# A gated two-branch linear-attention kernel: the raw K and Q weights loaded by one queue in the order of the fold steps

## The chip, the cores and the metric

The kernel runs on one core of a Trainium2 chip. Five engines work side by side, each through its own list of instructions in program order: TensorE (PE, matrix products into PSUM; PEld are its weight loads), VectorE (DVE), ScalarE (ACT), GpSimd (POOL) and SyncE (SP, which here only issues transfers). They meet at semaphores. Transfers are issued by SyncE or GpSimd, each into a queue of its own, and carried out by 16 DMA engines. The metric is the time of one execution in microseconds (us), taken as the median of several runs.

## The reference

Two attention branches A and B work on the same x, and a gate mixes their outputs. S is 2048, the model width 448, with 16 heads of 28. Cut to what matters:

```python
def branch(x, wqkv, w_phi, wo):
    q, k, v = split(x @ wqkv)                    # 16 heads of 28
    pq = einsum("bhsd,hdf->bhsf", q, w_phi)      # the same for pk with k
    phi_q = concat([softmax(pq), softmax(-pq)])  # the same for phi_k
    kv = einsum("bhsf,bhsd->bhfd", phi_k, v)
    z = einsum("bhsf->bhf", phi_k)
    num = einsum("bhqf,bhfd->bhqd", phi_q, kv)
    den = einsum("bhqf,bhf->bhq", phi_q, z) + 1e-6
    return (num / den).reshape(B, S, D) @ wo

g = sigmoid((x * gate_w).sum(-1, keepdims=True))
return g * branch(x, A...) + (1 - g) * branch(x, B...)
```

## The kernel before

**Tiling.** The 2048 rows are 16 tiles of 128; x arrives transposed in eight pairs of tiles. Every float32 operand of a projection is split into a high part (rounded to the matmul's input format) and a low part (what is left), and a projection of one tile and one branch is 11 matmuls: four of high by high, four of high x by low weight, three of low x by high weight. ACT (or GpSimd) makes the high part, VectorE or GpSimd the low part by a subtraction.

**Folding.** The feature map applies `w_phi` to q and k. The kernel multiplies `w_phi` into the K and Q weights once, at the start. That takes four fold steps n = 0 to 3: branch b = n // 2, and in it half gh of the heads. A step is 32 small matmuls into the PSUM tile F (line 357), a transpose of F by VectorE into the buffer `ft0` (in `ret`) for even n or `ft1` (in `ru`) for odd n (line 362), and then for K and for Q two high parts by ACT and two low parts by VectorE or GpSimd, into `rk` and `rq`. F is one buffer, so step n + 1 needs the transpose of step n; and the transpose of step n + 2 needs all eight parts of step n to be read.

**The raw K and Q weights** (`in_wkt`, `in_wqt`: 448 columns, of which the host repeats the last 64 to make 512) are loaded into `wts`, a view of `ret` with 28 of each 32 partitions in use. `load_wt(k, b)` loads both halves of a branch in four transfers, one for each group of 32 partitions: two are issued by SyncE, two by GpSimd. The branch B half of `wts` lies where the raw V weights (`wvr`) are, so it waits until these are split.

**The start.** TensorE runs some warm-up matmuls, then V of tiles 0 and 1 (line 441, `v_first`), which takes the parts of x pair 0 and of the V weights as they arrive. V of tile 1 goes into the PSUM tile K, for want of another. Then V of tiles 2 to 4 (line 409) is interleaved with the four fold steps, and K and Q of tile 0 follow. From there on a steady pattern of K, Q, V, the accumulation of kv, and later the output stage fills TensorE to the end.

**What sets the order.** `steps()` is a list by hand; it gives TensorE's order. All other instructions are placed by `Plan.order`: a list scheduler that takes, for the engine free next, the ready step with the earliest due time. A due time follows backwards from the steps that need it, less a handicap `ahead` that some steps are given. SyncE may have eight transfers under way: a ninth waits for the semaphore of the one eight places before it. Steps marked `two` are those of VectorE or GpSimd that the plan does not let run beside one of the other engine. Only the order is kept: on the chip each engine runs through its list and waits at semaphores.

The lines of the prediction's steps: 290 to 302 load and split x pair 0; 319 to 329 the V weights; 341 to 348 `load_wt`; 350 to 371 `fold`; 453 to 459 `v_out`, which evicts V and reads the gate column `glog`; 666 to 678 `later`, which hands the fold buffers over.

## Time and profile before

| | us |
|---|---|
| median of the 3 runs | 347.61 |
| lowest, highest run | 343.46, 347.83 |
| profiled execution, its own time | 345.97 |
| its span, first to last instruction | 344.2 |
| TensorE busy in the span | 333.1 (97%) |
| VectorE busy | 285.1 (83%) |
| GpSimd busy | 251.5 (73%) |
| ScalarE busy | 143.7 (42%) |

Busy times are of one profiled execution. A TensorE that is 97% busy need not be at its best, since a matmul counts as busy from its start to its modelled end, and they overlap: the distance from start to start says what one costs. A wait in brackets in the rows of a timeline is the time in which that engine stood idle just before, and what ended it.

### The profile page before, as it was taken

The page shows a single profiled execution, that of the slowest core. Times are in us where ns is not written, and L with a number is a line of the kernel's source. Part 1 is how long each engine was busy: PE and PEld are TensorE (multiplying, and loading weights), DVE is VectorE, ACT ScalarE, POOL GpSimd, SP SyncE. Part 2 cuts the span into 40 slices and gives each one's busy share as a digit, 9 for nine tenths or more (in the row PEclk, how much of TensorE's full clock was granted, in tenths as well). Part 3 has the DMA queues.
Part 4 walks back from the last instruction along what each step waited for, and adds up shares of the span by engine and source line. Part 5 has one row for each costly group of instructions (what it writes and reads, how often), then busy time and mean ns, then how long its engine had stood idle before and what let it go on. Part 6 is the DMA issues. An engine that isn't in the chain of part 4 may idle for free.

```text
span 344.2 us, 8900 instructions
## 1 busy us (share of the span) xinstructions
PE 333.1 (97%) x3776; PEld 296.5 (86%) x3776; DVE 285.1 (83%) x338; ACT 143.7 (42%) x219; POOL 251.5 (73%) x211
## 2 busy tenths in 40 slices
PE   7889899999999999999999999999999999999995
PEld 6777587999999999999999999899878888788894
DVE  4608886997779769899998999997599999999960
ACT  4516743553444535364444452343043243433231
POOL 8426605899999799999996998697087778788500
PEclk9999989999999999999999999999999999999999
DMA  7995620550317756964735422376974545141011
GB/s 251 251 206 133 203 75 1 156 168 2 116 55 261 252 169 229 327 204 197 246 84 236 143 55 81 96 248 261 301 259 164 202 152 183 76 177 55 29 53 53
DMA packets 29262, 55.18 MB, mean 160 GB/s; under 512 B 4472, under 2 KB 23528, under 8 KB 26920
## 3 DMA queue, kind: packets, MB, share of 16 engines
q1 hardware_dynamic: 28328, 52.68, 47.6%
q0 software_dynamic: 896, 1.95, 2.6%
q8 instruction: 29, 0.48, 0.6%
q14 instruction: 9, 0.07, 0.1%
HBM read 32.00 MB, written 24.22 MB: 163 GB/s over the span
## 4 chain that ended last, share of the span: by engine, by line
POOL 30%; PE 24%; DVE 23%; DMA 10%; issue 8%; ACT 2%; SPq 1%; POOLq 0%; DVEq 0%; ACTq 0%
POOL ret L266 20%; PE O L630 10%; DVE ret L545 5%; DMA ret<-in_wqt 4%; PE K L409 3%; POOL rx L266 3%; PE Q L409 3%; DVE rv L593 3%; POOL rv L602 3%; PE N L582 2%; DVE sm L488 2%; DVE mx L481 2%; DVE qsm L540 2%; DMA wst<-wos 1%; DMA ret<-in_wv 1%
## 5 line engine op out<-in xcount | busy, mean ns | idle before, releaser
L409 PE MATMUL K<-rk,rx 128*128 128x432 f32 x352 | 74.0, 366 | 0.7 <-ACT pk L269 0.6
L409 PE MATMUL Q<-rq,rx 128*128 128x432 f32 x352 | 72.4, 360 | 0.2 <-DVE Q L672 0.2
L409 PEld LDWEIGHTS K<-rk,rx 128*128 128x128 f32 x352 | 67.1, 192 | 5.1 <-ACT pk L269 1.5
L630 PE MATMUL O<-rk,rx 128*128 128x448 f32 x336 | 70.6, 369 | 0.1
L630 PEld LDWEIGHTS O<-rk,rx 128*128 128x128 f32 x336 | 62.5, 188 | 8.5 <-ACT rx L621 1.2
L409 PEld LDWEIGHTS Q<-rq,rx 128*128 128x128 f32 x352 | 65.9, 188 | 4.4 <-PE K L409 0.7
L269 ACT ACTIVATE ret<-ret 128x896 f32<-128x896 f32 x48 | 45.7, 953 | 55.0 <-POOL ret L266 54.9
L266 POOL TENSOR_TENSOR ret<-ret,sm 128x896 f32<-128x896 f32 x32 | 53.9, 1707 | 8.1 <-DVE sm L489 8.1
L266 POOL TENSOR_TENSOR ret<-pk,mx 128x896 f32<-128x896 f32 x16 | 27.3, 1705 | 16.6 <-DVE mx L481 16.5
L488 DVE TENSOR_REDUCE sm<-ret 128x32 f32<-128x896 f32 x32 | 33.8, 1073 | 6.7 <-ACT ret L269 6.7
L545 DVE STREAM_TRANSPOSE ret<-ret 128x2048 f32<-128x2048 f32 x16 | 36.5, 2282 | 1.9 <-POOL ret L266 1.6
L540 DVE TENSOR_REDUCE qsm<-ret 128x32 f32<-128x896 f32 x32 | 33.4, 1055 | 3.0 <-ACT ret L269 2.7
L409 PE MATMUL VA<-rv,rx 128*128 128x450 f32 x154 | 34.7, 372 | 0.3 <-POOL rx L266 0.3
L409 PE MATMUL VB<-rv,rx 128*128 128x448 f32 x154 | 33.7, 366 | 0.0
L266 POOL TENSOR_TENSOR ret<-qmn,ru 128x896 f32<-128x896 f32 x16 | 28.2, 1765 | 5.3 <-DVE ret L545 4.2
L269 ACT ACTIVATE ret<-ru 128x896 f32<-128x896 f32 x16 | 15.2, 952 | 39.4 <-issue 17.3
L409 PEld LDWEIGHTS VA<-rv,rx 128*128 128x128 f32 x154 | 28.5, 189 | 3.6 <-POOL rx L266 0.7
L409 PEld LDWEIGHTS VB<-rv,rx 128*128 128x128 f32 x154 | 28.8, 188 | 3.0 <-issue 0.4
L266 POOL TENSOR_TENSOR ret<-mx,pk 128x896 f32<-128x896 f32 x16 | 27.3, 1706 | 1.5 <-DVE mx L482 1.5
L266 POOL TENSOR_TENSOR ret<-ret,qsm 128x896 f32<-128x896 f32 x16 | 27.3, 1705 | 0.9
L602 POOL TENSOR_TENSOR rv<-rv,rd 128x896 f32<-128x896 f32 x14 | 23.8, 1703 | 1.1
L534 DVE TENSOR_REDUCE qmn<-ru 128x32 f32<-128x896 f32 x16 | 16.9, 1058 | 6.7 <-DMA ru<-qd 6.6
(94 smaller groups left out, 445.1 us busy)
## 6 DMA issues: line engine op xcount, KB each, us to landing
ed<-ret SPq DMA_DIRECT2D x8, 1024.0 KB
ret<-ed SPq DMA_DIRECT2D x8, 1024.0 KB
qd<-ru SPq DMA_DIRECT2D x64, 112.0 KB
ru<-qd SPq DMA_DIRECT2D x16, 448.0 KB
out<-ret SPq DMA_DIRECT2D x16, 224.0 KB
wod<-wst SPq DMA_DIRECT2D x14, 224.0 KB
rk<-wod SPq DMA_DIRECT2D x2, 1568.0 KB
xraw<-in_xt SPq DMA_DIRECT2D x6, 512.0 KB
```

The lines of the kernel that those rows point to most:

```text
L266: return lambda: ENG[eng].tensor_tensor(val(o), val(a), val(b), op)
L269: return lambda: A.activation(val(o), val(i), f, **k)
L409: nc.tensor.matmul(bank[name][:, k, lo:hi], x[:, xc, o:o + P], w[l][:, c], start=i == 0, stop=i == len(XT) - 1)
L481: put("DVE", 2 * D, lambda: V.tensor_reduce(mh[0], pkh, AX.X, OP.max), [kp], [km[0]])
L488: put("DVE", 2 * D, lambda s=s, e3=e3: V.tensor_reduce(sm[:, s], e3, AX.X, OP.add), [ke[s]], [("sm", t % 2, s)])
L534: put("DVE", 2 * D, lambda: V.tensor_reduce(qmn, tq.rearrange("p c b g f -> p c (b g) f"), AX.X, OP.min), [kt], [kn])
L540: put("DVE", 2 * D, lambda s=s, e3=e3: V.tensor_reduce(qsm[:, s], e3, AX.X, OP.add), [ke[s]], [("qsm", i, s)])
L545: add("DVE", 2.25, lambda: V.transpose(eTf[slot], eq.rearrange("p s a c f -> p (s a c f)")), ke, turned(slot))
L582: nc.tensor.matmul(bank["N"][32 * g:32 * g + 32, r, 2 * b * P:2 * b * P + 2 * P], kvt[32 * r:32 * r + 32, b, s, g], eTp[slots[0] // 2][32 ...
L593: add("DVE", 0.07 + 1.08 * nt, lambda: V.transpose(ctr().rearrange("p (r n) -> p r n", r=4), bank["N"][:, :, :2 * nt * P]), ["N"], [("ctr" ...
L602: put(eng, 2 * D, lambda: ENG[eng].tensor_tensor(mid["o", n % 3].rearrange("p (c a f) -> p a c f", c=4, a=8), ctv()[:, :, i, :, :DH], rd[: ...
L630: nc.tensor.matmul(bank[pb][:, 0, :D], a, w, start=i == 0, stop=i == len(terms) - 1)
```

## The change

It has five parts.

1. `load_wt` loads one fold step instead of one matrix of one branch: eight transfers (four groups of partitions in the order 0, 2, 1, 3, in each K and then Q) of 28 partitions, two heads' rows and 448 columns, all issued by SyncE. There are 32 of them where there were 16, and GpSimd issues none.
2. The 64 repeated columns are no longer loaded. GpSimd copies them, one copy for each step (`COPY ret<-ret`), which waits for all eight transfers of the step; the fold waits for the copy. Two memsets at the start clear those columns in the partitions that no transfer writes.
3. The V weights are loaded branch by branch (all of A, then all of B), by large `ahead` values; the low part of x pair 0 that GpSimd made goes to VectorE.
4. TensorE's order: each fold step comes one V group earlier, and V of tile 4, branch B, goes behind the first K.
5. The q low parts of all four steps go to GpSimd ("DP" in all); VectorE had those of steps 2 and 3. The transposes of all steps and the gate column of tiles 0 and 1 get an `ahead`; the `two` marks are set otherwise.

```diff
-    yield from (("V01", 0, 0, 1), ("x1",), ("V01", 1, 0), ("V01", 1, 1), ("wq", 0), ("x", 2), ("wq", 1), ("V", 2), ("F", 0, 0, "DP"), ("V", 3, 0), ("F", 0, 1, "DP"))
...
+    yield from (("V01", 0, 0, 1), ("x1",), ("V01", 1, 0), ("V01", 1, 1), ("wt", 0), ("x", 2), ("wt", 1), ("wt", 2), ("wt", 3), ("V", 2, 0), ("F", 0, "DP"), ("V", 2, 1))
...
-    def low_part(eng, n, o, a, h, r, w):
-        put(eng, n, tt(eng, o, a, h, OP.subtract), r, w, two=eng == "DVE")
+    def low_part(eng, n, o, a, h, r, w, **k):
+        put(eng, n, tt(eng, o, a, h, OP.subtract), r, w, two=True, **k)
...
-        low_part("POOL", 4 * P, t[:, 5:7], xraw[:, 1:3], f[:, 1:3], [("x0raw", 1), ("x0h", 1), ("x0h", 2)], [("x0l", i) for i in (1, 2)])
+        low_part("DVE", 4 * P, t[:, 5:7], xraw[:, 1:3], f[:, 1:3], [("x0raw", 1), ("x0h", 1), ("x0h", 2)], [("x0l", i) for i in (1, 2)], ahead=140.0)
...
-        add("SP", 0.4, dma(wvr[:, c, lo:hi], wv[c * P:(c + 1) * P, lo:hi]), [], [("wvr", c, b)], lat=2.5, kb=331, ahead=50.0 if c + b == 0 else 30.0 - 2 * (c + 4 * b))
+        add("SP", 0.4, dma(wvr[:, c, lo:hi], wv[c * P:(c + 1) * P, lo:hi]), [], [("wvr", c, b)], lat=2.5, kb=331, ahead=8000.0 if c + b == 0 else 6000.0 - 500 * (c + 4 * b))
...
-    def load_wt(k, b):
-        rows = (wkt, wqt)[k][b].rearrange("(q g d) c -> q d g c", q=4, d=DH)
-        for q in range(4):
-            o, i, w = wts[32 * q:32 * q + DH, k, b], rows[q], [("wt", k, b, q)]
-            if q < 2:
-                add("SP", 0.2, dma(o, i), [], w, lat=2, kb=690)
-            else:
-                add("POOL", 0.6, lambda o=o, i=i: G.dma_start(o, i), [("vh", 2, 1)], w, lat=4 + 1.3 * (4 * b + 2 * k + q - 2), ahead=8.0 if b == 0 else 0.0)
+    def load_wt(n):
+        b, gh = divmod(n, 2)
+        for q in (0, 2, 1, 3):
+            for k in range(2):
+                i = (wkt, wqt)[k][b].rearrange("(q l g d) c -> q g d l c", q=4, l=2, d=DH)[q, gh, :, :, :D]
+                o = wts[HP * q:HP * q + DH, k, b].rearrange("p (l g) c -> p g l c", l=2)[:, gh, :, :D]
+                add("SP", 0.33, dma(o, i), [], [("wt", k, n, q)], lat=2, kb=180, ahead=100.0 - 30 * n)
+        t = wts[:, :, b].rearrange("p k (l g) c -> p g k l c", l=2)[:, gh]
+        put("POOL", 256, lambda: G.tensor_copy(t[:, :, :, D:], t[:, :, :, 3 * P:D]), [("wt", k, n, q) for k in range(2) for q in range(4)], [("wd", n)], two=False, ahead=6.0)
...
-        add("PE", 1.4, mm, [("wpd",), *[("wt", k, b, q) for k in range(2) for q in range(4)]], ["F"])
+        add("PE", 1.4, mm, [("wpd",), ("wd", n), *[("wt", k, n, q) for k in range(2) for q in range(4)]], ["F"])
...
-            add("ACT", 0.2, act(glog[:, t:t + 1], lambda: bank[n_][:, k, D:D + 1], AF.Exp, scale=-1.0), [kb], [("gl", t)])
+            add("ACT", 0.2, act(glog[:, t:t + 1], lambda: bank[n_][:, k, D:D + 1], AF.Exp, scale=-1.0), [kb], [("gl", t)], ahead=9.0 * (t < 2))
...
+    for b in range(2):
+        first("POOL", 0.3, lambda b=b: G.memset(wts[:, :, b, :, 3 * P:D] if b == 0 else wts[:, 1, 1, 3, 3 * P:D], 0.0),
+              wt0 if b == 0 else [("wt", 1, 3, q) for q in range(4)])
```

What the plan makes of it, at three places. First TensorE's list from V of tile 2 to the second K, before. VA and VB are V of branches A and B, F is a fold step, K and Q are the projections; x11 is one group.

```order
L409 MATMUL VA<-rv,rx 128x450 x11
L409 MATMUL VB<-rv,rx 128x448 x11
L357 MATMUL F<-ret,wpd 32x256 x32
L409 MATMUL VA<-rv,rx 128x450 x11
L357 MATMUL F<-ret,wpd 32x256 x32
L409 MATMUL VB<-rv,rx 128x448 x11
L409 MATMUL VA<-rv,rx 128x450 x11
L357 MATMUL F<-ret,wpd 32x256 x32
L409 MATMUL VB<-rv,rx 128x448 x11
L357 MATMUL F<-ret,wpd 32x256 x32
L409 MATMUL K<-rk,rx 128x432 x11
L409 MATMUL Q<-rq,rx 128x432 x11
```

The same place in TensorE's list after the change:

```order
L410 MATMUL VA<-rv,rx 128x450 x11
L358 MATMUL F<-ret,wpd 32x256 x32
L410 MATMUL VB<-rv,rx 128x448 x11
L410 MATMUL VA<-rv,rx 128x450 x11
L358 MATMUL F<-ret,wpd 32x256 x32
L410 MATMUL VB<-rv,rx 128x448 x11
L358 MATMUL F<-ret,wpd 32x256 x32
L410 MATMUL VA<-rv,rx 128x450 x11
L358 MATMUL F<-ret,wpd 32x256 x32
L410 MATMUL K<-rk,rx 128x432 x11
L410 MATMUL VB<-rv,rx 128x448 x11
L410 MATMUL Q<-rq,rx 128x432 x11
```

One group of V stands ahead of the first fold step instead of two, one between steps 1 and 2 and between steps 2 and 3, and the last V group stands between the first K and the first Q.

Second, SyncE's list from x pair 1 (`ret<-in_xt`) to x pair 3, before. `in_wkt` and `in_wqt` are the raw K and Q weights, `xraw<-in_xt` x pairs 2 and 3; DMAHW0 to 7 are the semaphores of its eight places.

```order
L272 DMA ret<-in_xt 128x4x256 [waits DMAHW2_49]
L272 DMA ret<-in_wkt 28x4x512 [waits DMAHW3_49]
L272 DMA ret<-in_wkt 28x4x512 [waits DMAHW4_49]
L272 DMA ret<-in_wqt 28x4x512 [waits DMAHW5_49]
L272 DMA ret<-in_wqt 28x4x512 [waits DMAHW6_49]
L272 DMA xraw<-in_xt 128x4x256 [waits DVE_49,DMAHW7_49,Activation_49,Pool_49]
L272 DMA ret<-in_wkt 28x4x512 [waits DMAHW0_49,DVE_49]
L272 DMA ret<-in_wkt 28x4x512 [waits DMAHW1_49]
L272 DMA ret<-in_wqt 28x4x512 [waits DMAHW2_49,DVE_49]
L272 DMA ret<-in_wqt 28x4x512 [waits DMAHW3_49]
L272 DMA xraw<-in_xt 128x4x256 [waits DMAHW7_49,DMAHW4_49,Pool_49]
```

SyncE's list after the change, from x pair 1 to the first transfer of fold step 1; 23 more of the same kind follow, and then x pair 3:

```order
L272 DMA ret<-in_xt 128x4x256 [waits DMAHW2_49]
L272 DMA ret<-in_wkt 28x2x448 [waits DMAHW3_49,Pool_49]
L272 DMA ret<-in_wqt 28x2x448 [waits DMAHW4_49]
L272 DMA ret<-in_wkt 28x2x448 [waits DMAHW5_49]
L272 DMA ret<-in_wqt 28x2x448 [waits DMAHW6_49]
L272 DMA ret<-in_wkt 28x2x448 [waits DMAHW7_49]
L272 DMA ret<-in_wqt 28x2x448 [waits DMAHW0_49]
L272 DMA ret<-in_wkt 28x2x448 [waits DMAHW1_49]
L272 DMA ret<-in_wqt 28x2x448 [waits DMAHW2_49]
L272 DMA xraw<-in_xt 128x4x256 [waits DMAHW3_49,DVE_49,Activation_49]
L272 DMA ret<-in_wkt 28x2x448 [waits DMAHW4_49]
```

Ahead of x pair 2 stands one fold step instead of half a branch, the rest behind it; the last transfer of step 0 waits for DMAHW2, the semaphore of x pair 1.

Third, GpSimd's list from the splits of x pair 1 to the first q low parts, before (`rx<-ret` is x pair 1, `rx<-xraw` x pair 2, `rq` are q low parts; DMASW are the semaphores of its own queue):

```order
L266 TENSOR_TENSOR rx<-ret,rx 64x128 [waits DMAHW2_49,Activation_49,Pool_49]
L348 DMA ret<-in_wqt 28x4x512 [waits DMAHW4_49,DMAHW5_49,DMAHW1_49,DMAHW6_49,DMASW4_49,DVE_49]
L348 DMA ret<-in_wqt 28x4x512 [waits DMASW5_49]
L348 DMA ret<-in_wkt 28x4x512 [waits DMAHW3_49,DMAHW7_49,DMAHW0_49,DMASW6_49]
L348 DMA ret<-in_wkt 28x4x512 [waits DMASW7_49]
L266 TENSOR_TENSOR rx<-ret,rx 128x3x128 [waits Pool_49]
L314 CAST rx<-xraw 128x1024 [waits DMAHW7_49]
L266 TENSOR_TENSOR rx<-xraw,rx 64x256 [waits Pool_49]
L266 TENSOR_TENSOR rx<-xraw,rx 128x768 [waits Pool_49]
L678 MEMSET ret 128x64x4 [waits DMAHW5_49,DMASW1_49,DMAHW6_49,DMASW0_49,PE_49]
L678 MEMSET ret 128x64x4 [waits DMAHW3_49,DMAHW4_49,DMASW3_49,DMASW2_49]
L266 TENSOR_TENSOR rq<-ret,rq 128x2x8x27 [waits DVE_49,Activation_49]
```

GpSimd's list after the change, from the second split of x pair 1:

```order
L266 TENSOR_TENSOR rx<-ret,rx 128x3x128 [waits Pool_49]
L349 COPY ret<-ret 128x4x64 [waits DMAHW4_49,DMAHW5_49,DMAHW3_49,DMAHW6_49,DMAHW2_49,DMAHW7_49,DMAHW1_49,DMAHW0_49]
L314 CAST rx<-xraw 128x1024 [waits DMAHW3_49]
L266 TENSOR_TENSOR rx<-xraw,rx 64x256 [waits Pool_49]
L266 TENSOR_TENSOR rx<-xraw,rx 128x768 [waits Pool_49]
L349 COPY ret<-ret 128x4x64 [waits DMAHW4_49,DMAHW5_49,DMAHW3_49,DMAHW6_49,DMAHW2_49,DMAHW7_49,DMAHW1_49,DMAHW0_49]
L266 TENSOR_TENSOR rq<-ret,rq 128x2x8x27 [waits DVE_49,Activation_49]
L349 COPY ret<-ret 128x4x64 [waits DMAHW4_49,DMAHW5_49,DMAHW3_49,DMAHW6_49,DMAHW2_49,DMAHW7_49,DMAHW1_49,DMAHW0_49]
L266 TENSOR_TENSOR rq<-ret,rq 128x2x8x27 [waits Activation_49]
L683 MEMSET ret 128x64x4 [waits PE_49,Pool_49]
L683 MEMSET ret 128x64x4
L349 COPY ret<-ret 128x4x64 [waits DMAHW4_49,DMAHW5_49,DMAHW3_49,DMAHW6_49,DMAHW2_49,DMAHW7_49,DMAHW1_49,DMAHW0_49]
```

The transfers are gone from it, and the copies of steps 0 to 3 stand between its splits and the q low parts, each waiting for all eight semaphores of SyncE's places.

44 lines of the change are left out of this document (22 added, 22 removed).

## The prediction

> **What bounds the kernel now.** I read the busy time by stage first, then TensorE's timeline through the stage that the change touches, then who is late there. The stage view gives a stretch and its length, the busy time of TensorE, its weight loads, VectorE (DVE), ScalarE (ACT) and GpSimd (POOL), the granted TensorE clock, the DMA share and GB/s.
>
> ```profile
> 5.59:17.51 11.92, 9.89 (x53) 8.15 (x46) 8.14 (x13) 6.62 (x14) 7.32 (x14) 1.00 1.06 280
> 52.86:340.30 287.44, 286.99 (x3286) 258.98 (x3286) 252.79 (x302) 116.40 (x173) 227.29 (x173) 1.00 0.47 158
> ```
>
> From 52.86 to 340.30 TensorE is busy for 286.99 of 287.44 us: nothing is to be had there except by starting it earlier. What can be won lies ahead of it. In TensorE's timeline (start, length, what, in brackets the wait before it) VA and VB hold V of the two branches, and F is a fold step:
>
> ```profile
> 5.59 0.47 PE L441 MATMUL VA<-rv,rx 128*128 128x450 f32 x1
> ...
> 9.05 0.47 PE L441 MATMUL VA<-rv,rx 128*128 128x450 f32 x1 [1.13 <-DVE rv L266]
> ...
> 15.14 2.53 PE L441 MATMUL K<-rv,rx 128*128 128x448 f32 x11 [0.74 <-ACT glog L269]
> 17.51 2.40 PE L409 MATMUL VA<-rv,rx 128*128 128x450 f32 x11
> 19.74 2.38 PE L409 MATMUL VB<-rv,rx 128*128 128x448 f32 x11
> 22.06 0.61 PE L357 MATMUL F<-ret,wpd 28*32 28x256 f32 x2
> 23.54 1.69 PE L357 MATMUL F<-ret,wpd 28*32 28x256 f32 x62 [0.86 <-DMA ret<-in_wqt]
> 25.15 2.50 PE L409 MATMUL VA<-rv,rx 128*128 128x450 f32 x11
> ...
> 35.73 2.49 PE L409 MATMUL VB<-rv,rx 128*128 128x448 f32 x11
> 39.88 1.49 PE L357 MATMUL F<-ret,wpd 28*32 28x256 f32 x64 [1.66 <-DVE ret L362]
> 41.31 3.98 PE L409 MATMUL K<-rk,rx 128*128 128x432 f32 x11
> 45.51 2.40 PE L409 MATMUL Q<-rq,rx 128*128 128x432 f32 x11 [0.23 <-DVE Q L672]
> 47.75 0.36 PE L409 MATMUL K<-rk,rx 128*128 128x432 f32 x1
> ```
>
> Starts are pipelined, so prices go from start to start. Eleven V matmuls cost 19.74 - 17.51 = 2.23, say 2.25; a fold step 41.31 - 39.88 = 1.43; eleven K or Q matmuls 47.75 - 45.51 = 2.24. From 5.59 to 47.75 stand ten groups of V (four of them for tiles 0 and 1), four fold steps, one K and one Q: 22.5 + 5.7 + 4.5 = 32.7 us of work in 42.16 us. So 9.5 us are lost, 2.9 in the first V stage (11.92 for 9.0) and 6.6 behind it. That is the ceiling of any gain: 345.97 - 9.5 = 336.5.
>
> **Where the 6.6 sit.** Fold step 0 took 25.15 - 22.06 = 3.09, 1.66 too much, for a Q weight that had not landed. Fold step 3 came 1.9 late (39.88 - 35.73 - 2.25), since the transpose ahead of it waited for GpSimd. The next K took 4.20 instead of 2.24. The rest is small pieces.
>
> ```profile
> 29.08 1.04 POOL L314 CAST rx<-xraw 128x1024 fp32r<-128x1024 f32 x1 [9.79 <-DMA xraw<-in_xt]
> ```
> ```profile
> 37.51 2.32 DVE L362 STREAM_TRANSPOSE ret<-F 128x2048 f32<-128x2048 f32 x1 [1.26 <-POOL rq L266]
> ```
>
> GpSimd sat 9.79 us for x pair 2 (tiles 4 and 5), whose transfer stood among the fold weights, so its q low parts came late, and the transpose could not overwrite what they still read. The root is the order and speed of the transfers:
>
> ```profile
> 6.00:11.00 5.00, 3.71 (x18) 2.77 (x17) 4.45 (x6) 3.48 (x6) 4.72 (x9) 1.00 1.07 363
> 11.00:13.00 2.00, 2.00 (x11) 1.85 (x10) 1.25 (x3) 0.99 (x4) 0.00 (x0) 1.00 1.05 200
> 11.00:29.00 18.00, 16.39 (x189) 13.02 (x187) 5.60 (x8) 6.16 (x15) 3.92 (x6) 1.00 1.02 210
> 29.00:31.00 2.00, 2.00 (x18) 1.81 (x11) 1.90 (x2) 2.00 (x5) 1.84 (x2) 1.00 0.84 168
> ```
>
> **The change part by part: transfers.** Loads over 128 partitions ran at 363 GB/s up to 11 us; fold weights and x pair 2 at 210, the DMA engines full (share 1.02); the tail, with few transfers left, at 168 (0.84). The change loads 448 of 512 columns: 32 transfers of 28 x 2 x 448 x 4 bytes = 100 KB, 3.21 MB instead of 3.67, all from SyncE, in the order step 0 (0.80 MB), x pair 2 (0.52), steps 1, 2, 3. What SyncE's queue reaches alone is not shown. I bound it by 168 and 210 and take 210: a share of 1.02 says that the engines, not the number of queues, set it, and at 200 (11 to 13) it was no different. Counted from 11.0: step 0 at 14.8, x pair 2 at 17.3, step 1 at 21.1, step 2 at 24.9, step 3 at 28.8. Only step 0 is held up: its last transfer reuses the semaphore of x pair 1.
>
> ```profile
> 13.88 1.15 ACT L269 ACTIVATE rx<-ret 128x512 fp32r<-128x512 f32 x2 [0.37 <-DMA ret<-in_xt]
> ```
> ```profile
> 8.09 0.93 SPq L272 DMA_DIRECT2D ret<-in_wqt  x2
> ...
> 33.47 0.39 SPq L272 DMA_DIRECT2D xraw<-in_xt  x1
> ```
>
> x pair 1 landed at 13.88, so that transfer is issued at 14 and lands near 16. An issue costs 0.93 / 2 = 0.47; the 25 behind it take 11.7 us, to 25.7, less than the transfers. x pair 3 and the output weights stand behind them on SyncE; they were issued from 33.47 on, and the queue now reaches them before 29. The prices that follow are from the view of one tile (count, then min/median/max in ns):
>
> ```profile
> L266 DVE TENSOR_TENSOR rv<-ret,rv x8: 618/624/2172, 4.8 to 13.0; 128x450 fp32r<-128x450 f32 x4, 128x448 fp32r<-128x448 f32 x4
> ...
> L269 ACT ACTIVATE rk<-ret x4: 937/968/1007, 28.1 to 40.7; 128x432 fp32r<-128x432 f32 x4
> L266 DVE TENSOR_TENSOR rk<-ret,rk x4: 920/1062/1821, 29.1 to 44.4; 128x432 fp32r<-128x432 f32 x4
> ...
> L266 POOL TENSOR_TENSOR rx<-ret,rx x2: 573/792/1012, 15.2 to 18.3; 64x128 fp32r<-64x128 f32 x1, 128x384 fp32r<-128x384 f32 x1
> ...
> L678 POOL MEMSET ret<- x2: 312/313/314, 33.4 to 33.6; 128x256 f32 x2
> L266 POOL TENSOR_TENSOR rq<-ret,rq x2: 1575/1814/2052, 33.9 to 35.4; 128x432 fp32r<-128x432 f32 x2
> ```
>
> The eight transfers taken off GpSimd were issued ahead of its wait of 9.79 us: what they took there is no gain. Its new memsets of unread columns (0.31 for 256 elements, so some 0.8) delay the w_phi transfers at the start, whose product is wanted at 17: no loss.
>
> **First V stage.** The wait of 1.13 was for the low part of 2.17 us; the other seven took 0.62. GpSimd was splitting x meanwhile:
>
> ```profile
> 7.21 1.29 POOL L266 TENSOR_TENSOR rx<-xraw,rx 128x512 fp32r<-128x512 f32 x1
> ```
>
> That split moves to VectorE, where 512 columns cost about 0.65. The low parts of tiles 0 and 1 are then ready just ahead of TensorE, the branch order brings the last weight of branch A one transfer earlier, and reading the gate column ahead of the evictions removes the 0.74. I leave 0.4 of the 2.9: the stage ends at 5.59 + 9.0 + 0.4 = 15.0 instead of 17.51.
>
> **Fold stage, walked.** V 2A 15.0 to 17.25. Fold 0: data at 16, but the copy of the repeated columns stands behind GpSimd's two splits of x pair 1 (0.57 + 1.01 after ACT's second half), to 17.4. The copy's price is not in the trace; the memset of 256 elements at 0.31 and the cast of 1024 at 1.04 bound it, and I take 0.3, the memset's size. Only the ninth of 32 matmuls needs it, so 0.2 is lost: fold 0 ends at 18.9. V 2B to 21.15, V 3A to 23.4, fold 1 (data 21.1, copied by 22.3 behind the splits of x pair 2) to 24.8, V 3B to 27.1, fold 2 (data 24.9) to 28.5, V 4A to 30.8. Fold 3 needs the transpose of fold 2, which stands behind a k low part: ACT evicts V 3B to 27.7 and splits to 28.6, VectorE subtracts to 29.5 and transposes (2.32) to 31.8. So 1.0 is lost; fold 3 runs to 33.3, K to 35.5, V 4B to 37.7, Q to 39.9. GpSimd's queue there is q low part, copy 2, q low part, two memsets, copy 3, two q low parts; at 1.6 to 1.8 each it is done by 32.6, before the transpose of fold 3 wants their buffer at 33.4. The last four q low parts, now all GpSimd's, take 4 x 1.8 and end before its softmax work begins. The second K would start at 39.9 instead of 47.75, 7.85 earlier. A k low part can be held up by GpSimd (1.82 against 0.92); I take off 0.25 for that. The gain is 7.6.
>
> On this hold-up the Trainium skill, page SBUF — State Buffer, section Who interferes with whom, says that a VectorE instruction with two SBUF inputs is shut out for the whole of a GpSimd instruction that reads SBUF. By that rule the two low parts ahead of the last transpose could each lose up to a subtraction's length, and I estimate 0.6 to 1 us less gain.
>
> **The sum.** 345.97 (the span 344.2 and 1.8 around it) - 7.6 = 338.4. The profiled execution lies 1.64 below the median of the runs, 347.61, and inside their 343.46 to 347.83; from the median it would be 340.0.
>
> **Half clock.** 1.7 of the 7.6 is the K that took 4.20, and that was the clock:
>
> ```profile
> 38.30:41.70 3.40, 1.82 (x66) 1.21 (x67) 3.37 (x3) 2.35 (x4) 1.76 (x2) 1.00 0.51 156
> 41.70:45.10 3.40, 3.40 (x11) 2.82 (x9) 3.08 (x3) 1.44 (x2) 0.00 (x0) 0.50 0.64 178
> ```
>
> After a stretch with TensorE busy for 1.82 of 3.40 us the clock was 0.50 for the next 3.40. In my walk no such stretch has more than 1.0 idle, so I let it go. The Trainium skill, page TensorE: Matmul & The Clock Gate, Part 1, has the clock halve after a whole idle window of about 3.4 us. By that rule the wait of 1.66 us is not the cause, and taking it away need not help. The trace speaks against it: no such window was wholly idle here.
>
> **Rivals.** (a) One queue is too slow. At 168 GB/s step 2 lands at 28.5 and step 3 at 33.2; copy 3 holds the q low parts of fold 1 to 36.8, the transpose of fold 3 ends at 39.1, the second K starts at 42.4: gain 5.35, or 3.65 if the idle time halves the clock, so 340.6 to 342.3. For it the row at 168, against it the full engines at 210. (b) The half clock comes anyway: gain 5.9, 340.1. (c) The earlier start is lost again behind 52.86, since VectorE (252.79 of 287.44) and GpSimd (227.29) are close behind TensorE: about 345. Against it: their work there follows from TensorE's first K, and its order stays. (d) Slower: the single queue falls so far behind that fold 3 comes later than now. In (a) the second K follows step 3's data by 9.2 us; it comes later than 47.75 only if 3.73 MB last until 38.55, under 135 GB/s, and 2% are lost under 108. The lowest full row is 168. Time: 348 to 355.
>
> **How the numbers follow.** The walk 0.60, (a) 0.18, (b) 0.08, (c) 0.10, (d) 0.04. The range from 336.4 (the ceiling) to 342.4 (the end of (a)) leaves out (c), (d) and a little more. Two per cent, about what a measurement here can tell from no change, is 340.7 from the median and 339.1 from the profiled execution. Most of the walk lies below it, (a), (b) and (c) above. Faster 0.57, within 0.39, slower 0.04.
>
> **What would show it.** TensorE's second K near 40 (right) or after 42 (a); the first V stage ending near 15.0; fold 0 starting near 17.3; GB/s from 14 to 29 near 210; no clock of 0.50 near 40. I would be wrong if GpSimd's copies wait for data while the q low parts behind them hold the transposes, or if the gain at the second K is not found at the end.

## The result, and the profile after

| | kernel before | changed kernel |
|---|---|---|
| median of 20 runs each | 345.27 us | 342.05 us |
| lowest to highest | 342.74 to 350.38 | 340.52 to 344.17 |
| profiled execution, time and span | 345.97, 344.2 | 342.14, 340.4 |
| start of the second K, from the span's start | 47.75 | 41.45 |

The changed kernel takes 0.9906 of the time before, 95% interval 0.9881 to 0.9931: 3.2 us less. 7.6 was forecast, from the profiled execution of the kernel before. The stage view of the changed kernel, with the columns of the prediction's first fence, has the first V stage, the stretch from there to the second K, and the stretch behind it:

```profile
6.26:15.84 9.58, 9.29 (x53) 8.30 (x45) 6.34 (x13) 6.63 (x14) 1.68 (x8) 1.00 0.89 271
15.84:41.45 25.61, 25.14 (x345) 20.19 (x344) 17.90 (x14) 15.06 (x24) 15.29 (x16) 1.00 0.75 205
46.56:336.91 290.35, 287.98 (x3286) 258.75 (x3286) 253.18 (x302) 116.21 (x173) 227.25 (x173) 1.00 0.47 156
```

The first two are almost full. The third is the stretch that ran from 52.86 to 340.30 before, the same 3286 matmuls in 290.35 us instead of 287.44. So 2.9 us came into the part that was taken for full: idle 2.4 instead of 0.45, and 1.0 of longer busy time. TensorE's timeline up to the second K:

```profile
6.26 0.47 PE L442 MATMUL VA<-rv,rx 128*128 128x450 f32 x1
...
15.84 2.39 PE L410 MATMUL VA<-rv,rx 128*128 128x450 f32 x11
18.16 1.50 PE L358 MATMUL F<-ret,wpd 28*32 28x256 f32 x64
19.59 2.49 PE L410 MATMUL VB<-rv,rx 128*128 128x448 f32 x11
...
24.25 1.50 PE L358 MATMUL F<-ret,wpd 28*32 28x256 f32 x64
25.67 2.49 PE L410 MATMUL VB<-rv,rx 128*128 128x448 f32 x11
28.15 1.79 PE L358 MATMUL F<-ret,wpd 28*32 28x256 f32 x64
29.87 2.50 PE L410 MATMUL VA<-rv,rx 128*128 128x450 f32 x11
32.83 1.79 PE L358 MATMUL F<-ret,wpd 28*32 28x256 f32 x64 [0.46 <-DVE ret L363]
34.55 2.44 PE L410 MATMUL K<-rk,rx 128*128 128x432 f32 x11
36.83 2.37 PE L410 MATMUL VB<-rv,rx 128*128 128x448 f32 x11
39.22 2.40 PE L410 MATMUL Q<-rq,rx 128*128 128x432 f32 x11
41.45 4.47 PE L410 MATMUL K<-rk,rx 128*128 128x432 f32 x22
```

No fold step waits for a transfer any more, the one wait left is for a transpose, and the K behind fold step 3 takes 36.83 - 34.55 = 2.28 at full clock instead of 4.20. The second K starts 6.30 earlier. Much later, where the numerators (N) stand between Q and the output matmuls (O), the changed kernel's timeline reads:

```profile
234.10 4.59 PE L410 MATMUL Q<-rq,rx 128*128 128x432 f32 x22
238.63 2.71 PE L583 MATMUL N<-ret,kvt 32*32 32x256 f32 x123
242.31 0.62 PE L583 MATMUL N<-ret,kvt 32*32 32x256 f32 x5 [0.98 <-issue]
242.87 4.60 PE L410 MATMUL Q<-rq,rx 128*128 128x432 f32 x22
247.40 2.16 PE L583 MATMUL N<-ret,kvt 32*32 32x256 f32 x100
250.15 0.71 PE L583 MATMUL N<-ret,kvt 32*32 32x256 f32 x28 [0.59 <-issue]
250.80 8.83 PE L631 MATMUL O<-rk,rx 128*128 128x448 f32 x42
```

and that of the kernel before:

```profile
239.39 4.59 PE L409 MATMUL Q<-rq,rx 128*128 128x432 f32 x22
243.91 2.75 PE L582 MATMUL N<-ret,kvt 32*32 32x256 f32 x128
246.60 4.59 PE L409 MATMUL Q<-rq,rx 128*128 128x432 f32 x22
251.12 2.75 PE L582 MATMUL N<-ret,kvt 32*32 32x256 f32 x128
253.81 8.40 PE L630 MATMUL O<-rk,rx 128*128 128x448 f32 x39
```

The lead is 239.39 - 234.10 = 5.29 at the first row and 253.81 - 250.80 = 3.01 at the last. Two pauses, 0.98 and 0.59 us, stand inside the N groups; "issue" says that TensorE waited for nothing that the profile shows. With what stands around them they cost 5.29 - 3.01 = 2.3 us. The waits of TensorE behind the second K, summed (us in all, times, longest), name the rest:

```profile
PE N L583 <- issue: 1.6, 2, 1.0
PE K L410 <- ACT pk L269: 0.6, 1, 0.6
PE T L501 <- POOL ret L266: 0.4, 2, 0.2
PE Q L410 <- DVE ru L266: 0.3, 1, 0.3
```

The K row stood there before as well. Matched instruction by instruction, the lead is 6.30 at the second K, 5.73 at 66.8 us (most of that loss at T, which waits for GpSimd), 5.29 from 208 on (Q waits for VectorE's `ru`), 3.01 behind the N groups, 3.39 at the last O and 3.8 at the end of the span.

### The profile page after: what moved, and what is told of

Read it like the earlier page. It is cut to its first block, busy times and chain, and to the rows that moved or that the text cites. A ratio compares the mean times of both kernels' runs of the same rounds, so it can differ in the third digit from the quotient of the medians.

```text
span 340.4 us, 8927 instructions
## 1 busy us (share of the span) xinstructions
PE 332.1 (98%) x3776; PEld 296.1 (87%) x3776; DVE 279.6 (82%) x335; ACT 143.3 (42%) x219; POOL 252.2 (74%) x212
## 4 chain that ended last, share of the span: by engine, by line
PE 44%; POOL 24%; DVE 14%; issue 9%; DMA 5%; ACT 3%; SPq 1%; POOLq 0%; DVEq 0%; ACTq 0%
PE O L631 21%; POOL ret L266 20%; PE N L583 7%; PE Q L410 5%; PE VB L410 3%; POOL rx L266 3%; PE K L410 3%; DVE ret L546 3%; DVE sm L489 2%; PE VA L410 2%; DVE mx L482 2%; DMA ed<-ret 2%; DMA ret<-in_wv 2%; PE F L358 1%; ACT ret L269 1%
## 5 line engine op out<-in xcount | busy, mean ns | idle before, releaser
L410 PE MATMUL K<-rk,rx 128*128 128x432 f32 x352 | 72.5, 360 | 0.7 <-ACT pk L269 0.6
L410 PEld LDWEIGHTS K<-rk,rx 128*128 128x128 f32 x352 | 65.7, 188 | 5.1 <-ACT pk L269 1.5
L583 PE MATMUL N<-ret,kvt 32*32 32x256 f32 x1024 | 22.7, 385 | 1.6 <-issue 1.6
```

The lines of the kernel that those rows point to most:

```text
L410: nc.tensor.matmul(bank[name][:, k, lo:hi], x[:, xc, o:o + P], w[l][:, c], start=i == 0, stop=i == len(XT) - 1)
L583: nc.tensor.matmul(bank["N"][32 * g:32 * g + 32, r, 2 * b * P:2 * b * P + 2 * P], kvt[32 * r:32 * r + 32, b, s, g], eTp[slots[0] // 2][32 ...
```

## The experiments

**What stops TensorE in the numerators?** The profile's page has a queue for instructions:

```profile
q8 instruction: 29, 0.48, 0.6%
```

29 packets of 16 KB for TensorE's 2 x 3776 instructions: one for some 260. That q8 is TensorE's is read from this count; with 92 more instructions of TensorE, in a run below, it has 30 packets. The 128 N matmuls with their 128 weight loads use one up in 2.7 us. Where these packets stand against SyncE's fetches of `ed` (1 MB each) is in the transfers of two windows, 234.0 to 239.9 and 239.9 to 242.4, of the changed kernel:

```profile
q1 hardware_dynamic: 694, 1.57, 86.4%
...
q1 hardware_dynamic: 543, 0.85, 93.5%
q8 instruction: 1, 0.02, 2.3%
```

No instruction packet in the first, one in the second; by the records of single transfers it started at 240.1. In the kernel before the packet of the same place started at 242.0, 2.6 us behind the start of Q, when the fetches of `ed` had just been issued (241.13, 1.74 behind Q). In the changed kernel they were issued 0.74 behind Q. SyncE's list in both, after and before (`qd` are four stores ahead of the fetches):

```profile
232.27 1.97 SPq L272 DMA_DIRECT2D qd<-ru  x4
...
234.84 0.86 SPq L272 DMA_DIRECT2D ret<-ed  x2
```
```profile
237.55 2.90 SPq L272 DMA_DIRECT2D qd<-ru  x4
...
241.13 0.82 SPq L272 DMA_DIRECT2D ret<-ed  x2
```

Theory A was that the packet now comes behind the fetches; theory B that the pauses were chance. Both kernels were run again first.

The changed kernel again, no edit:

> The changed kernel once more. Theory A (the two pauses of TensorE in the numerator matmuls, 0.98 us at 242.3 and 0.59 us at 250.1, come from its instruction packets of 16 KB, which arrive late because 1 MB fetches of ed got onto the DMA engines first): both pauses are there again within 0.3 us, since the order of the instructions and of the transfers is the same; time 342.0 to 342.3. Theory B (they were chance of one execution): the second profile has none, and is some 1.5 to 2.3 us shorter behind 238 us. The first V matmul starts at 5.6 to 6.3 us, by where in the warm-up the clock rises.

342.29 us, ratio 0.9912 (0.9883 to 0.9940). Both pauses were there, 1.26 and 0.39 us, at the same matmuls (behind the 123rd and the 100th); the packet started at 241.2, 6.1 us behind Q. So they are no chance.

The kernel before again, no edit:

> The kernel before once more. Theory A: no pause over 0.3 us in the numerator matmuls in a second profile either, and the fetch of instructions in the Q of tile 14 starts again at the same time as the fetches of ed or ahead of them. Theory B: a pause may stand here as well. If the K of 4.20 us at half clock is a matter of every run, the granted clock of most runs is near 0.995; if it comes and goes, the runs fall into two groups some 1.7 us apart. Time 345.3, ratio 1.000 +- 0.003.

346.47 us, ratio 1.0021 (0.9992 to 1.0049). No pause; the packet again 2.6 us behind Q. The K at half clock was there again. But TensorE waited 0.98 us for `ru` at the Q of 214.65, where the first profile had nothing: that wait is not the change's.

The fetches of `ed` moved behind the gate loads, in the changed kernel:

```diff
 def fetch(k, slot):
-    add("SP", 0.4, dma(eTf[slot], ed[k]), [("ed", k)], turned(slot), lat=3, kb=1048)
+    add("SP", 0.4, dma(eTf[slot], ed[k]), [("ed", k), *([("ga", 12, r) for r in range(4)] if slot > 1 and k < 2 else [])], turned(slot), lat=3, kb=1048)
```

> The changed kernel with the first two 1 MB fetches of ed issued behind the four gate loads, some 3 us later. Theory A: the instruction packet of about 236.7 us now comes before them, the pause of 0.98 us goes, Q of tile 15 starts 1.0 to 1.5 us earlier; the second pause of 0.59 us stays, since the third fetch of ed is not moved. Time 340.5 to 341.2, 1.0 to 1.5 us under the changed kernel. Theory B: no difference, 342.0 +- 0.4. If the numerator of the second pair now waits for ed (due at 247.4, its data estimated to land at 244.5), the gain is given back there and a wait for DMA shows it.

341.26 us, ratio 0.9881 (0.9848 to 0.9913). The transfers between 234.2 and 238.8 now hold the packet (it started at 236.8, 2.5 behind Q), and the timeline has no "issue":

```profile
q8 instruction: 1, 0.02, 1.3%
```
```profile
238.79 2.76 PE L583 MATMUL N<-ret,kvt 32*32 32x256 f32 x128
241.48 4.60 PE L410 MATMUL Q<-rq,rx 128*128 128x432 f32 x22
247.26 2.75 PE L583 MATMUL N<-ret,kvt 32*32 32x256 f32 x128 [1.18 <-DMA ret<-ed]
```

The second pause, expected to stay, went too, with the third fetch issued 0.6 instead of 0.1 us behind the Q of tile 15; the price was a wait of 1.18 for the data of `ed`.

The packets moved instead of the fetches, by more instructions at the start:

```diff
-WARM, SMALL = 10, 30
+WARM, SMALL = 9, 54
```

> The changed kernel with one large warm-up matmul replaced by 24 small ones: 46 more TensorE instructions, the same warm-up within 0.2 us, and every later instruction stands 46 places further in its 16 KB packet. Theory A: each packet is asked for 46 instructions earlier in the program, the one of the first pause at 234.1 instead of 236.7 us, ahead of the fetches of ed, and that pause goes (1.0 to 1.5 us less), the second one too if its packet then comes ahead of the third fetch of ed (2.3 us less in all, 339.7 to 341.0); a new pause may stand where another packet now meets a large transfer. Theory B: 342.0 +- 0.4, and pauses at places that have nothing to do with the packets.

340.77 us, ratio 0.9869 (0.9840 to 0.9899), against 342.29 for the changed kernel on the same chip. Both pauses went:

```profile
240.10 2.76 PE L583 MATMUL N<-ret,kvt 32*32 32x256 f32 x128
242.79 4.60 PE L410 MATMUL Q<-rq,rx 128*128 128x432 f32 x22
247.32 2.76 PE L583 MATMUL N<-ret,kvt 32*32 32x256 f32 x128
```

The count was wrong, though: the trace has 92 instructions more, since a matmul here runs as two (itself and its weight load), and the packet came 14 places earlier in the program, not 46, and 1.2 us behind Q. That was enough to be ahead of the data of `ed`. Of the 2.3 us won this profile gave 0.8 back at the Q of 209 us, which waited 1.05 for `ru` instead of 0.27.

The two mirror cases, with the kernel before. Fewer instructions:

```diff
-WARM, SMALL = 10, 30
+WARM, SMALL = 11, 7
```

> The kernel before with 23 of the small warm-up matmuls replaced by one large one: the same warm-up within 0.2 us, but 44 TensorE instructions fewer, so that each 16 KB packet of instructions is asked for 44 instructions later in the program. Theory A: the packet that came at 242.0 us in the kernel before, together with the first fetches of ed (issued from 241.13), is now asked for some 2 us later, behind them; the numerator matmuls pause 0.5 to 2 us as they do in the changed kernel, and the time rises by 0.5 to 2 us over the kernel before. Theory B (the packets have nothing to do with it): no pause, 345.2 +- 0.6.

347.23 us, ratio 1.0055 (1.0012 to 1.0097), but no pause: the packet came 0.1 us behind Q, earlier and not later. So it tested nothing of the theory; the place of a packet doesn't follow the count one for one. Most of the time lost went into a wait of 1.7 us for `ru`.

More instructions, as in the shifted kernel (`WARM, SMALL = 9, 54`):

> The kernel before with the same 46 instructions more that took the pauses out of the changed kernel. Theory A: its packets come ahead of the fetches of ed with or without them, no pause before and none now: 345.2 +- 0.6, so that the changed kernel with the shift stands 4.3 us, not 3.2 us, under the kernel before at the same places in the packets. Rival: the shift shortens both kernels alike (340.8 against 344.0), and the pause had no part in what the change lost.

346.55 us, ratio 1.0055 (1.0010 to 1.0101): no pause, and no gain, but a time above the expected 345.2 +- 0.6; the first V stage ended at 20.14 and the second K came at 48.52. The shift shortened only the kernel that has the pauses. The fetches of `ed` were issued 0.76 us behind Q here, as near as in the changed kernel, with the packet at 0.70.

The fetches of `ed` moved ahead in the kernel before:

```diff
-    yield from (("load_wo",), ("V", 14, 1), ("Q", 13), ("V", 15), ("free_v",), ("free_k",), ("kv", 14, 15), ("free_e",), ("kv_turn",), ("gates", 12, NT))
-    yield from (("fetch", 0, 2), ("fetch", 1, 3), ("Q", 14))
+    yield from (("load_wo",), ("V", 14, 1), ("q", 13, 0), ("q", 13, 1), ("V", 15), ("free_v",), ("free_k",), ("kv", 14, 15), ("free_e",), ("kv_turn",), ("fetch", 0, 2), ("fetch", 1, 3), ("qf", 13), ("gates", 12, NT))
+    yield "Q", 14
...
-                ku, [("qd", k, c)], lat=2.2, kb=160)
+                ku + ([("edf", 0), ("edf", 1)] if k == 13 and c > 1 else []), [("qd", k, c)], lat=2.2, kb=160)
...
-        add("SP", 0.4, dma(eTf[slot], ed[k]), [("ed", k)], turned(slot), lat=3, kb=1048)
+        add("SP", 0.4, dma(eTf[slot], ed[k]), [("ed", k)], [*turned(slot), ("edf", k)], lat=3, kb=1048)
...
-        add("SP", 0.4, dma(gd[:, lo:hi], gl), kl, [("gd", lo)], lat=2)
+        add("SP", 0.4, dma(gd[:, lo:hi], gl), kl + ([("edf", 0), ("edf", 1)] if lo else []), [("gd", lo)], lat=2)
```

> The kernel before with the first two 1 MB fetches of ed issued ahead of two of the qd stores and of the gate transfers, at about 239.5 instead of 241.13 us, on the same place of the instruction packets. Theory A: the packet that TensorE gets at 242.0 us (2.6 us behind the start of the Q of tile 14) now stands behind them and arrives 2 to 4 us later; the numerator matmuls that follow pause for 0.5 to 2.5 us, as in the changed kernel, with nothing of the change in it. Theory B: no pause there. Behind it the gate loads and the Q of tile 13 are later as well, so the time itself is not used.

One execution, 350.65 us. The fetches were issued 0.32 us behind Q, the packet came at 246.7, 5.6 behind Q, and the kernel before has pauses at nearly the same places as the changed kernel (behind the 126th and the 104th matmul):

```profile
245.67 2.74 PE L582 MATMUL N<-ret,kvt 32*32 32x256 f32 x126
249.08 0.59 PE L582 MATMUL N<-ret,kvt 32*32 32x256 f32 x2 [0.68 <-issue]
249.60 4.60 PE L409 MATMUL Q<-rq,rx 128*128 128x432 f32 x22
254.13 2.55 PE L582 MATMUL N<-ret,kvt 32*32 32x256 f32 x104
258.07 0.70 PE L582 MATMUL N<-ret,kvt 32*32 32x256 f32 x24 [1.39 <-issue]
```

Theory A holds in both directions. In the three profiles with pauses the packet started 5.2 to 5.3 us behind the issue of the first fetch of `ed`; in the fourteen others it started ahead of that issue or at most 0.84 us behind it. And in all six pauses TensorE went on 2.2 to 2.5 us behind the start of the late packet (242.31 - 240.10 and 250.15 - 247.73 in the changed kernel). The Trainium skill, page DMA: Bandwidth & Descriptors, section Queues, rings and completion order, says that a DMA engine serves its queues in turn but drains a whole packet of one before it turns to the next. A fetch of 1 MB takes an estimated 2.8 us at the 378 GB/s that the changed kernel moved from 238.6 to 242.3, and the instruction packet came 3.3 us later than with the gate loads first (240.1 against 236.8): the trace agrees, if what one fetch lays on an engine is one packet, which no run here shows.

**Why does the second K come at 41.5 to 43.6, not at 39.9?** First the parts. The part on the first V stage taken back, in the shifted kernel:

```diff
-        low_part("DVE", 4 * P, t[:, 5:7], xraw[:, 1:3], f[:, 1:3], [("x0raw", 1), ("x0h", 1), ("x0h", 2)], [("x0l", i) for i in (1, 2)], ahead=140.0)
+        low_part("POOL", 4 * P, t[:, 5:7], xraw[:, 1:3], f[:, 1:3], [("x0raw", 1), ("x0h", 1), ("x0h", 2)], [("x0l", i) for i in (1, 2)], ahead=140.0)
...
-            add("ACT", 0.2, act(glog[:, t:t + 1], lambda: bank[n_][:, k, D:D + 1], AF.Exp, scale=-1.0), [kb], [("gl", t)], ahead=9.0 * (t < 2))
+            add("ACT", 0.2, act(glog[:, t:t + 1], lambda: bank[n_][:, k, D:D + 1], AF.Exp, scale=-1.0), [kb], [("gl", t)])
```

> The shifted changed kernel with the part on the first V stage taken back: the low part of x0's chunks 1 and 2 on GpSimd again, glog not put ahead. If that part was worth what was said of it, the 2.17 us low part and the wait of 0.74 us for glog are back, V of tile 2 starts at 17.2 to 17.8 instead of 16.1 us, second K at 43.2 to 43.9 instead of 42.1, and the time is 1.0 to 1.8 us longer (341.8 to 342.6). Rival: the fold steps wait for their transfers anyway, the second K comes at 42.1 +- 0.4 and the time is 340.8 +- 0.5.

343.49 us, ratio 0.9931 (0.9896 to 0.9965). V of tile 2 started at 17.69 and the second K at 43.50: 1.4 later than in the shifted kernel, of which 1.19 is the wait for `glog`; no low part of 2.17 us came back. The second K of the shifted kernel itself came anywhere from 41.92 to 43.61 in its three profiles, so one profile alone would not carry this; but the kernel that follows, on the same chip and with this part, took 342.08, also 1.4 less. The part is worth about 1.4 us.

The copies taken out and all 512 columns loaded, in the shifted kernel (the fold's wait for the copy goes too):

```diff
-                i = (wkt, wqt)[k][b].rearrange("(q l g d) c -> q g d l c", q=4, l=2, d=DH)[q, gh, :, :, :D]
-                o = wts[HP * q:HP * q + DH, k, b].rearrange("p (l g) c -> p g l c", l=2)[:, gh, :, :D]
+                i = (wkt, wqt)[k][b].rearrange("(q l g d) c -> q g d l c", q=4, l=2, d=DH)[q, gh]
+                o = wts[HP * q:HP * q + DH, k, b].rearrange("p (l g) c -> p g l c", l=2)[:, gh]
...
-        put("POOL", 256, lambda: G.tensor_copy(t[:, :, :, D:], t[:, :, :, 3 * P:D]), [("wt", k, n, q) for k in range(2) for q in range(4)], [("wd", n)], two=False, ahead=6.0)
...
```

> The shifted changed kernel (46 instructions more) with all 512 columns loaded and no copies by GpSimd: 14% more bytes in the same number of packets. If SyncE's queue goes by packets (118 a microsecond, whatever their size), the loads land at the same times as with 448 columns and nothing changes: second K at 42.1 +- 0.4, 340.8 +- 0.5. If it goes by bytes (210 GB/s), each step takes 0.55 us more and the last lands 2.2 us later, near 32 us, still ahead of its fold step at 32.8 to 33.6: the time is then the same as well or at most 0.5 us longer. Either way the copies gain nothing on the path; longer by over 1 us would say that they do.

342.08 us, ratio 0.9916 (0.9884 to 0.9948), with the second K at 42.19 and a span of 339.9 like the shifted kernel's. From 20 to 30 us the DMA engines moved 219 to 227 GB/s, and no fold step waited for a load. Since the median was of another chip, both ran side by side once more.

> The shifted kernel with all 512 columns loaded and no copies by GpSimd, beside the shifted kernel on one chip. If the copies gain nothing on the path (fold steps never waited for the loads in the profile, second K at 42.2 with and without), the two medians agree within 0.6 us. Rival: the 14% more bytes hold up something behind the fold steps, and this kernel is 1.0 to 1.6 us slower, as the medians of two chips had it.

> The shifted kernel as the measure for the other two, third time: 340.7 to 341.8, no pause in the numerator matmuls, V of tile 2 9.2 to 9.5 us behind ScalarE's start on the second chunk of V weights, wherever that lands.

340.72 us (0.9848, 0.9814 to 0.9882) without copies, 341.50 (0.9885, 0.9843 to 0.9927) with them: the copies gain nothing. The two are 0.8 apart, a little more than the 0.6 expected, and the other way round. The profile without copies has no pause and no wait for `ru` (1.22 in the one with them); against the first profile of the kernel before it was 6.15 us ahead at the second K and still 5.92 at the last O.

The shifted kernel ran once more beside the next two.

> The changed kernel with the 24 small warm-up matmuls more (one large one less) once again, beside the three others of this call. Theory A: again no pause in the numerator matmuls, 340.5 to 341.6. Theory B: pauses of 0.3 us or more are there in this execution, and the time is 342.0 +- 0.5.

341.71 us (0.9864, 0.9824 to 0.9903), no pause. Its first V stage was the slowest so far among the kernels that keep that part, up to 17.17, and shows why. ScalarE's timeline of the changed kernel, then of this run (its start on the second chunk of V weights), then TensorE's of this run:

```profile
6.36 0.58 ACT L269 ACTIVATE rv<-ret 128x450 fp32r<-128x450 f32 x1 [1.23 <-DMA ret<-in_wv]
```
```profile
7.85 2.49 ACT L269 ACTIVATE rv<-ret 128x450 fp32r<-128x450 f32 x4 [2.78 <-DMA ret<-in_wv]
```
```profile
8.48 0.47 PE L442 MATMUL VA<-rv,rx 128*128 128x450 f32 x1 [1.16 <-ACT rv L269]
```

TensorE started at 6.2 to 6.3 in both; the weights came 1.5 later, and V of tile 2 1.33 later. Over ten profiles with this stage that V starts 9.2 to 9.5 us behind ScalarE's start on that chunk, which lies between 6.36 and 7.85. Ending the warm-up earlier should then do nothing, and it was tried:

```diff
-WARM, SMALL = 9, 54
+WARM, SMALL = 6, 57
```

> The same with 6 large and 57 small warm-up matmuls instead of 9 and 54 (the same number of TensorE instructions): the warm-up ends some 1.3 us earlier, at about 5.2 us, so the first V matmul starts on its data at 5.3 to 5.6 us in every execution instead of at 5.6 to 6.5. If the start of that stage is worth its length (the reading by which 0.67 us of the missing gain lie there), V of tile 2 starts at 15.2 to 15.6 us, the second K at 41.3 to 41.6, and the time is 0.5 to 0.9 us under the kernel with 9 and 54. Rival: the stage waits for its V weights instead, or half of it runs at the lower clock, and the second K stays at 42.1 +- 0.3.

341.13 us (0.9857, 0.9814 to 0.9899). The first V matmul started at 5.28, the second K at 42.30, as in the shifted kernel: a wait of 0.9 for the V weights took the time. The rival was right.

That chunk brought ahead of the rest of x0, in the kernel with the short warm-up:

```diff
-        for i, (lo, hi) in enumerate(((0, 1), (1, 4))):
+        for i, (lo, hi) in enumerate(((0, 1), (1, 2), (2, 4))):
             if i:
-                load_wv(0, 0)
+                load_wv(i - 1, 0)
...
-        put("DVE", 6 * P, lambda: V.tensor_copy(t[:, 1:4], xraw[:, 1:]), [("x0raw", 1)], [("x0h", i) for i in (1, 2, 3)], ahead=160.0)
+        put("DVE", 2 * P, lambda: V.tensor_copy(t[:, 1], xraw[:, 1]), [("x0raw", 1)], [("x0h", 1)], ahead=160.0)
+        put("DVE", 4 * P, lambda: V.tensor_copy(t[:, 2:4], xraw[:, 2:]), [("x0raw", 2)], [("x0h", i) for i in (2, 3)], ahead=155.0)
...
```

> The kernel with the short warm-up (6 large, 57 small) and x0 loaded in three parts instead of two: chunk 0, chunk 1, then the second V weights (chunk 1), and only behind them chunks 2 and 3 of x0 (256 KB, estimated 0.7 us at the 370 GB/s of that stretch). If the end of the first V stage hangs on the landing of that second chunk of V weights, ScalarE starts on it at 5.8 to 6.8 us instead of 6.4 to 7.9, V of tile 2 starts some 9.3 us behind it, at 15.1 to 16.1 us, the second K at 41.0 to 42.0 us, and the time is 0.4 to 0.9 us under the shifted kernel (340.2 to 340.9 if that is at 341.2). Rival: the third chunk of x0 or of V is late instead, a wait for it takes the place of the other, V of tile 2 stays at 16.2 +- 0.3 us and the time within 0.4 us.

342.14 us (0.9902, 0.9866 to 0.9937). The chunk came at 6.63, no earlier than in the better runs, the third came at 8.36, and the waits moved: 1.2 for V weights and 0.6 for x0 instead of 0.9. V of tile 2 came at 17.21 and the second K at 43.28, and the time was 0.6 us over that of the shifted kernel beside it. The rival had the mechanism right, a wait in place of the other, but not the price: it had V of tile 2 at 16.2 +- 0.3 and the time within 0.4. Neither order of these loads shortened the stage.

**The wait of T for GpSimd.** Every profile of the changed kernel loses 0.35 us there. VectorE's minimum of the second key tile put later, in the shifted kernel:

```diff
-put("DVE", 2 * D, lambda: V.tensor_reduce(mh[1], pkh, AX.X, OP.min), [kp], [km[1]])
+put("DVE", 2 * D, lambda: V.tensor_reduce(mh[1], pkh, AX.X, OP.min), [kp], [km[1]], ahead={1: -4.0, 2: 0.0}.get(t, 0.0))
```

> The shifted kernel with VectorE's minimum of the second key tile put behind its sums, as in the kernel before, so that GpSimd gets the four factors earlier. If the 0.35 us that every profile of the changed kernel loses at the T of tiles 0 and 1 (start near 64.7 us, a wait for GpSimd) come from that order, the wait goes and what is gained stays to the end: 0.2 to 0.4 us less. Rival: GpSimd is full there (14.6 us of work from 47.8 us on) and the wait stays within 0.15 us; the time is the same within 0.5 us either way.

341.60 us (0.9853, 0.9810 to 0.9896). The wait grew, from 0.4 to 0.7 in all, so this step being early is not its cause. The edit does not give back the order of the kernel before as a whole, since other sums of VectorE moved too; what makes T wait stays open.

## Why the prediction was wrong, point by point

The step that failed is "nothing is to be had there except by starting it earlier", read the other way round: that an earlier start is kept to the end. Of the 6.30 us won at the second K, 2.9 were gone at the last O: 2.28 went at the two pauses, 0.57 mostly at T and 0.44 at the Q that waits for `ru`, and 0.38 came back later. In outcome this is part of rival (c), which had a chance of 0.10 and was set aside because "their work there follows from TensorE's first K, and its order stays". Its mechanism was another, though: neither VectorE nor GpSimd made the pauses. In the changed kernel SyncE's fetches of `ed` were issued 0.74 instead of 1.74 us behind Q, ahead of an instruction packet. No row of the profile before could have shown the pause itself; the neighbours of the packet were there to be read.

That the earlier start brought the fetches nearer is not shown, and it looks like bad luck. The first of the four stores of `qd` is issued 1.83 and 1.84 us ahead of Q in the two kernels alike. By the records of single issues, one of the four took 1.41 us in the kernel before (0.30 to 0.43 the others), while an instruction packet that started at 238.5 was under way; in the changed kernel that packet started at 231.6, ahead of the stores, and none of the four took over 0.61. And the kernel before with the instructions shifted has its fetches 0.76 us behind Q, at the old start. What decides, as far as these runs show, is how the instruction packets fall among SyncE's transfers, and moving some instructions at the start changes that too.

The other two losses are smaller. The wait for `ru` comes and goes in the kernel before as well (none, none, 0.98, 0.98 and 1.7 us in its five profiles; none to 1.22 in the twelve of the changed kernel and its variants), so how much of it is the change's stays open. So does the cause of the wait for GpSimd at T. (VectorE's order did change near 50 us; the one edit to it made that wait longer.)

The sum, term by term, between the two profiled executions: 7.85 forecast at the second K, less 0.84 (first stage), less 0.71 (walk), less 2.91 (behind it), plus 0.44 that the end behind the last O was shorter, is 3.83, the difference of the spans. That 342.05 lies inside the stated range is luck: its upper end was set by rival (a), which did not come.

- **First V stage, 15.0.** 15.84, and 15.8 to 17.2 over the runs that keep this part. What was removed went: the wait for `glog` and the long low part. The 0.4 left for the rest was too little: the stage took 9.58, and what its end follows is now the landing of the second chunk of V weights. The 0.67 us that the first V matmul started later (6.26 against 5.59) were not the cause, as the short warm-up shows.
- **The first stage's worth in the kernel before.** 2.5 of the 2.9 us lost there were counted as a gain. In the kernel before itself that stage ended anywhere from 17.4 to 21.8 in its profiles, variants included, while the second K stayed at 47.75 to 48.5, since a late end of the stage only took the place of waits behind it (with 21.8 no fold step waited). In the changed kernel the stage is on the path, as taking its part back showed.
- **Transfers, 210 GB/s.** Right. SyncE's queue alone moved 216 GB/s from 18 to 24 us; step 0's last transfer was issued at 13.63, held by x pair 1 as said, and no fold step waited for data. Rivals (a) and (d) fall.
- **The copies, 0.3 each.** 0.40 three times, and 0.96 once:

```profile
29.86 0.96 POOL L349 COPY ret<-ret 128x256 f32<-128x256 f32 x1 [1.09 <-DMA ret<-in_wkt]
```

  All off the path; so is the whole part, since 512 columns without a copy take the same time.
- **The walk, 24.9 from V of tile 2 to the second K.** 25.61. Fold steps 2 and 3 took 1.72 each from start to start instead of 1.43 (0.58 in all), which was not foreseen; the transpose behind the k low part cost 0.7 (32.83 - 29.87 - 2.25) where 1.0 was set down. Of the two low parts ahead of the last transpose one took 1.93 instead of 0.93, beside GpSimd's low parts, and the other 0.95. That fits in size the rule of the Trainium skill, page SBUF — State Buffer, section Who interferes with whom. But K waited for neither, so the 0.6 to 1 us less that was estimated by it did not come.
- **The half clock, 1.7.** It went, as said, but the clock alone was not worth 1.7. All five profiles of the kernel before, with its variants, have one stretch of 3.41 us at 0.50; none of the twelve of the changed kernel has one ahead of the end. In two of the five it came earlier, at 18.25 and 16.57, and the K behind fold step 3 ran at full clock. Then Q waited 1.54 and 1.34 us for VectorE, and from the first K to the second it took 6.38 and 6.01 us instead of 6.44. That of the 18.25, the kernel before with fewer instructions:

```profile
41.74 2.60 PE L409 MATMUL K<-rk,rx 128*128 128x432 f32 x11
45.88 2.40 PE L409 MATMUL Q<-rq,rx 128*128 128x432 f32 x11 [1.54 <-DVE Q L672]
```

  So the clock alone was worth 0.1 to 0.4 there. In the changed kernel Q did not wait: a V group stands between K and Q, and VectorE's memset of Q has a larger `ahead`; which of these did it is not tested. In the kernel before, run again (stage view):

```profile
37.32:40.72 3.40, 1.60 (x60) 1.01 (x65) 3.35 (x3) 1.58 (x3) 2.54 (x2) 1.00 0.51 153
40.72:44.13 3.41, 3.41 (x38) 2.48 (x8) 3.21 (x2) 2.20 (x3) 0.00 (x0) 0.50 0.62 193
```

  With 1.60 of 3.40 us busy the clock still halved, so the whole idle window that the Trainium skill's page TensorE: Matmul & The Clock Gate, Part 1, names is more than the clock needed here. Rival (b) falls.

With the instructions shifted the changed kernel took 340.8, 341.7 and 341.5 us in three tries, under the 342.1 and 342.3 of the changed kernel and the 345.1 to 346.5 of the kernel before. The lowest median, 340.7, is that of the shifted kernel without copies.

## What to carry to other kernels

An earlier start reaches the end only if nothing along the way moves against something else, and the instruction stream is one of the things that move: before counting a shift as kept, look where large transfers stand against the fetches of instructions in the dense matmul stretches behind it. A stall called "issue" in the middle of many small matmuls is a reason to look for an instruction packet that came late; here, issuing the large transfers some 3 us later, or 92 more instructions at the start, took it out. A loss that a later wait hides is worth nothing until that wait is gone, and then all of it.

## What the runs showed of the hardware

- TensorE's instructions come in 16 KB packets over the same DMA engines as the data. With two 1 MB fetches ahead of one it came 3.3 us later, and TensorE stood idle for 0.39 to 1.39 us twice, in each of three profiles; in both profiles of the changed kernel behind the same matmuls.
- SyncE's own issues get longer beside such a packet: over all 17 profiles 128 of the 440 issues that overlap one took over 0.9 us, and 18 of the 2977 others.
- How far a packet moves does not follow the number of instructions put ahead of it: 92 more moved it 14 places, 88 fewer moved it 24 places the same way.
- The same loads at the start land up to 1.5 us apart from run to run (6.36 to 7.85 us for the second chunk of V weights), in kernels with the same transfers up to there.
